# Weight magnitudes on VectorE, new due times, and a second layer turned by VectorE

## The chip, the cores and the metric

One core of one Trainium2 chip runs the whole program. The metric is device time in microseconds of one launch. TensorE (PE) multiplies, VectorE (DVE) and ScalarE (ACT) work elementwise, GpSimd (POOL) does some of the same more slowly, and SyncE (SP) issues most transfers. PEld is TensorE's weight load, which lies beside the multiplication.

## What is computed

A chunked attention, then two two-layer networks over its output, all in fp32 (3072 tokens, width 512, hidden width 2048):

```python
x = attention(q, k, v, mem_k, mem_v)      # chunks of 32, 16 keys to the left, 8 to the right, 8 memory keys
h = x @ moe_w_in                          # 3072 x 512 x 2048
y = softplus(h) @ moe_w_out               # 3072 x 2048 x 512
h = y @ moe2_w_in
out = prelu(h, alpha) @ moe2_w_out        # max(h, 0) + alpha * min(h, 0)
```

The weights arrive as 64-bit floats, seen as pairs of 32-bit words.

## The kernel before

**Three products for one.** Each fp32 operand is split into a high part (fp32r, a rounding copy by ACT) and a low part (the difference, by DVE or POOL). A product is then high*high + high*low + low*high, so that each 128x128x512 block is three matmuls.

**First network** (`schedule`, from line 814). Tokens go in six blocks `b` of 512, the hidden width in 16 slices `f` of 128. A step (b, f) is twelve matmuls `pe_h` into `ps_hh`, softplus on ACT (`act_first`, tile `ta`), the split `high`/`low` (tile `g`), and twelve matmuls `pe_out` into four banks `ps_o`. `SEGMENTS` (line 49) takes blocks 0 and 1 in alternation over slices 0-3, 4-7 and 8-15, so that weights need to be there only as they are used; at the end of a segment the four banks are copied out (`drain_one`, two by ACT and two by DVE, tile `o_sb`) before the next segment's first `pe_out`. Each weight slice comes in two halves of 128x512. A half is loaded (`load_raw`, three `raw` buffers), its magnitude is taken (`magnitude`, ACT function Abs, from the upper words, which lie at a stride of two), it is clamped and turned into fp32 bits by DVE (`clamp`, `convert_a`, `convert_b`, `convert_c`, tile `word`, three buffers), and split by ACT (`high_w`) and POOL (`low_w`) into `wsplit`. The weights of the second network go through the same four steps, also in this stage, and are written to DRAM as operands and sums (`in_ops`, `out_ops`). The attention of 24 tiles of 128 tokens is spread over the stage.

**Order.** All of this is put in order by a planner (`Plan`, lines 84 to 159): every piece has an engine, an assumed duration, what it comes after, the buffers that it takes and gives back, and a due time. Due times are offsets `O` (line 81) from the time of the step that needs the piece. The order that comes out is binding on each engine (`InOrder`, line 60).

**Second network** (`pairs`, line 798). Token blocks go in three pairs `p`. The products of a pair's two halves are made by a Strassen-Winograd scheme of seven products for eight. For each pair, `quad` runs eight times (q = 0 to 7, seven products of six matmuls each, PReLU by ACT and DVE, results `G[0..3, q]`), then `second` runs 56 units n (seven passes of eight). A unit is six matmuls from `g2[n]`, the split of one `G`, into two banks (m = 0, 1). `ready(n)` makes the split: an ACT cast (`high`) and a DVE subtraction (`low`). Its buffers are two of tag `g` and, for every third unit, one of the three `raw` buffers (line 475). In the last quad, `ahead` makes the units 0 to 2 (line 801); unit n makes unit n+2 (line 764). After a pass DVE or ACT put the sums and differences of the banks into `u` and `c` (`after`, line 719). In pairs 0 and 1, POOL adds some `G` by accumulating transfers (`SUMS`); in the last pair DVE adds them. `todo` holds the operands of the next pair, made by DVE and ACT.

**Turning.** A result `c` has hidden outputs on the partitions and tokens along the free axis. `turn` (line 683) transposes it on PE: eight 128x128 transposes into two `acc` banks, one copy by ACT, one by DVE, one transfer of 512 KB. It runs after units 39, 46 and 52, and for the fourth result in the first quad of the next pair (`between`) or, in the last pair, at the end of the program. SP issues in order: `load_w_in` at units 48 and 52 stands behind the output transfers of units 46 and 52.

Of the kernel before, what the change touches and what calls it, by code (L numbers as in the profile page):

```python
# [7 lines left out]
F32 = mybir.dt.float32  # L8
# [8 lines left out]
P = 128  # L17
# [37 lines left out]

A11, A12, A22, S1, S2, S3, S4 = range(7)
# [24 lines left out]
O = {'qo': 32.4, 'km': 28.62, 's': 30.88, 'm': 13.72, 'c': 0.72, 'e': 22.73, 'n': 0.37, 'r': 12.8, 'w': 16.33, 't': 1.22, 'pt': 5.93, 'v': -5.17, 'xh': -11.56, 'xl': 15.24, 'first': 3.34, 'gap': 5.43, 'second': 6.51, 'gap2': 14.3, 'raw': 15.77, 'ab': 7.61, 'cl': 10.42, 'ca': 1.59, 'cb': 4.8, 'cc': -3.37, 'wh': -8.57, 'wl': -26.27, 'odd': 20.31, 'sp': 22.46, 'hi': -4.71, 'lo': 5.91, 'out': 18.4, 'wait': 0.07, 'sloads': 34.06}  # L81
# [81 lines left out]
def attention_mlp_mlp_kernel(ctx: ExitStack, tc, qk, v, w1, w2, consts, out):  # L163
# [473 lines left out]

    def quad(p, q, between, ahead):
# [27 lines left out]
        n0 = halves_of(x1, G[0, q])  # L666
        product(p, n, S4, B22, x4, False)
# [3 lines left out]
        n1 = negative(G[1, q], f0)  # L671
        product(p, n, A22, T4, x3, False)
        prelu(G[1, q], n1, G[1, q])
        dve.scalar_tensor_tensor(out=G[1, q], in0=G[1, q], scalar=-1.0, in1=G[0, q], op0=ALU.mult, op1=ALU.subtract)
        n2 = halves_of(x3, G[2, q])
        minus_prelu(n2, f1, G[2, q])
# [6 lines left out]
    def turn(c, b, d):  # L683

        o = rpool.tile([P, 4, HK], F32, tag="raw", name="o_sb")
        for e in range(2):
            ps = bank(ps_acc, "acc")
            for j in range(2):
                for m in range(2):
                    tok = (2 * e + j) * P  # L690
                    pe.transpose(ps[:, j * HK + m * P:j * HK + (m + 1) * P], c[:, m, tok:tok + P], ident)
            if e:
                dve.tensor_copy(o[:, 2:4, :], ps.rearrange("p (j n) -> p j n", j=2))
            else:
                act.copy(out=o[:, 0:2, :], in_=ps.rearrange("p (j n) -> p j n", j=2))
        sp.dma_start(
            out=out[b * N2:(b + 1) * N2, d * HK:(d + 1) * HK].rearrange("(j p) n -> p j n", p=P), in_=o,
        )

# [5 lines left out]
    def second(p, todo):  # L705

        ps_of, kept, c, later, sums_now = {}, {}, {}, [], []
# [32 lines left out]
        for n in range(7 * NQ):  # L740
# [6 lines left out]
            for m in range(2):  # L747
                for k, (a, e) in enumerate(((0, 0), (0, 1), (1, 0))):
# [32 lines left out]
        return lambda: turn(c.pop((1, 0)), 2 * p, 1)  # L781
# [16 lines left out]
    def pairs(between):  # L798
# [5 lines left out]
        between()  # L804
# [12 lines left out]
    def schedule(when):  # L817
# [13 lines left out]
        for n, k in enumerate(order):  # L831
# [3 lines left out]
            add(("ab", n), "ACT", 0.62, need - O["ab"], lambda k=k: magnitude(0, k), [("raw", n)] + ([("ab", n - 1)] if n else []), ["word"])  # L835
# [89 lines left out]
        for j in range(4 * NQ):  # L925
# [3 lines left out]
            add(("ab2", j), "ACT", 0.62, due - 1, lambda j=j: magnitude(1, halves[j]), [("raw2", j)] + ([("ab2", j - 1)] if j else []), ["word"])  # L929
# [127 lines left out]
```

## Time and profile before

| | us |
|---|---|
| median of 3 runs | 1124.35 (1124.09 to 1126.4) |
| the profiled execution | 1125.37 |
| its span, first to last instruction | 1123.6 |
| TensorE busy | 1079.4 (96%) |
| ScalarE busy | 709.9 (63%) |
| VectorE busy | 686.0 (61%) |
| GpSimd busy | 216.3 (19%) |

The mean granted TensorE clock is 0.988 of full speed. A PE that is counted busy is not PE at its full rate: matmuls are pipelined, so the distance from one start to the next tells the rate. The span falls into the start (attention and the first weights, to about 200 us), the rest of the first network (to 643 us), and the second network (to the end). The rows below are read in that light.

### The profile page before, as it was taken

The numbers are of one execution on the slowest core, as the hardware profiler recorded it, in microseconds if no ns is written. First come the engines' busy times: TensorE is split into PE (matmuls) and PEld (weight loads), VectorE is DVE, ScalarE is ACT, GpSimd is POOL, SyncE is SP. The second block draws the span as 40 slices with busy tenths as digits, with TensorE's granted clock in tenths as the row PEclk, the third lists the DMA queues.
The fourth block names the chain that finished last, engine by engine and source line by source line (L and its number), as shares of the span: only waits on it lengthen the run. The fifth ranks groups of instructions, "written<-read, shape, count | busy, mean of one in ns | idle before, by whom it ended". The sixth has DMA issues, their size and how long they took to land.

```text
span 1123.6 us, 16444 instructions
## 1 busy us (share of the span) xinstructions
PE 1079.4 (96%) x6048; PEld 884.7 (79%) x6048; DVE 686.0 (61%) x1098; ACT 709.9 (63%) x1156; POOL 216.3 (19%) x244
## 2 busy tenths in 40 slices
PE   4798889999999999999999999999999999999998
PEld 3677677888888888888888888788888788888786
DVE  5788876545544543445257256778566768566874
ACT  4789888676766766656566455665455655456543
POOL 0233333333223233333333300000000000000000
PEclk9899989999999999999999999999999999999999
DMA  9864466868666654744446483898565997746802
GB/s 252 259 174 155 153 166 125 194 161 201 177 167 159 177 162 135 209 151 159 132 139 219 145 307 109 314 277 279 191 259 174 352 289 242 263 172 263 323 3 73
DMA packets 157600, 220.83 MB, mean 197 GB/s; under 512 B 73680, under 2 KB 108624, under 8 KB 150608
## 3 DMA queue, kind: packets, MB, share of 16 engines
q1 hardware_dynamic: 153488, 203.00, 55.5%
q0 software_dynamic: 4032, 16.78, 7.8%
q8 instruction: 48, 0.79, 0.3%
q14 instruction: 32, 0.26, 0.1%
HBM read 161.03 MB, written 46.14 MB: 184 GB/s over the span
## 4 chain that ended last, share of the span: by engine, by line
PE 79%; DVE 8%; ACT 7%; DMA 3%; issue 2%; SPq 0%; DVEq 0%; ACTq 0%
PE ps_q L68 35%; PE ps_o L68 20%; PE ps_hh L68 20%; DVE word L68 3%; DMA qk<-in_qk_dram 2%; ACT L68 2%; PE ps_s L68 2%; DVE gb L68 2%; ACT tp L68 2%; PE ps_x L68 2%; DVE g L68 1%; DMA raw<-in_w_dram 1%; ACT g L68 1%; ACT word L68 1%; PE ps_t L68 1%
## 5 line engine op out<-in xcount | busy, mean ns | idle before, releaser
L68 PE MATMUL ps_o<-g,wsplit 128*128 128x512 f32 x1152 | 284.2, 396 | 12.4 <-DVE o_sb L68 9.5
L68 PE MATMUL ps_hh<-x,wsplit 128*128 128x512 f32 x1152 | 283.4, 395 | 1.3 <-DVE x L68 0.8
L68 PEld LDWEIGHTS ps_o<-g,wsplit 128*128 128x128 f32 x1152 | 216.7, 190 | 60.2 <-ACT o_sb L68 10.7
L68 PEld LDWEIGHTS ps_hh<-x,wsplit 128*128 128x128 f32 x1152 | 215.4, 189 | 48.2 <-DVE x L68 1.8
L68 PE MATMUL ps_q<-g,wout 128*128 128x512 f32 x1008 | 233.3, 391 | 2.5 <-DVE g L68 2.3
L68 PE MATMUL ps_q<-xop,win 128*128 128x512 f32 x1008 | 229.7, 389 | 0.0
L68 PEld LDWEIGHTS ps_q<-g,wout 128*128 128x128 f32 x1008 | 188.0, 188 | 43.7 <-DVE g L68 4.5
L68 PEld LDWEIGHTS ps_q<-xop,win 128*128 128x128 f32 x1008 | 189.0, 188 | 39.2
L68 ACT ACT_TABLE_LOAD x120 | 154.0, 1283 | 10.7 <-DVE g L68 6.4
L68 ACT CAST g<-gb 128x512 fp32r<-128x512 f32 x168 | 100.3, 623 | 87.2 <-PE ps_q L68 71.6
L68 DVE TENSOR_TENSOR g<-ta,g 128x512 fp32r<-128x512 f32 x96 | 74.0, 771 | 130.3 <-ACT g L68 129.7
L68 DVE TENSOR_TENSOR g<-gb,g 128x512 fp32r<-128x512 f32 x168 | 113.4, 688 | 45.4 <-ACT g L68 44.5
L68 DVE TENSOR_SCALAR word<-word 128x512 f32<-128x512 f32 (+1 forms) x128 | 63.4, 495 | 89.0 <-ACT word L68 87.4
L68 DVE SCALAR_TENSOR_TENSOR word<-raw,word 128x512 int32<-128x512 int32 x128 | 108.2, 845 | 3.5
L68 ACT CAST g<-ta 128x512 fp32r<-128x512 f32 x96 | 59.3, 618 | 61.6 <-PE ps_o L68 61.1
L68 ACT ACTIVATE ta<-ps_hh 128x512 f32<-128x512 f32 x96 | 57.5, 599 | 59.9 <-PE ps_hh L68 55.2
L68 ACT ACTIVATE tp<-gb 128x512 f32<-128x512 f32 x48 | 30.4, 633 | 90.2 <-DVE gb L68 90.2
L68 POOL TENSOR_TENSOR wst<-wsum,wst 128x512 fp32r<-128x512 f32 x32 | 42.8, 1340 | 136.5 <-ACT wst L68 130.5
L68 DVE SCALAR_TENSOR_TENSOR gb<-gb,tp 128x512 f32<-128x512 f32 x48 | 33.2, 693 | 49.2 <-ACT tp L68 49.2
L68 POOL DMA_DIRECT2D gb<-gb x12 | 10.5, 874 | 267.7 <-DVE g L68 259.6
L68 POOL TENSOR_TENSOR wsplit<-word,wsplit 128x512 fp32r<-128x512 f32 x32 | 45.1, 1413 | 87.5 <-ACT wsplit L68 77.3
L68 POOL TENSOR_TENSOR wst<-word,wst 128x512 fp32r<-128x512 f32 (+1 forms) x32 | 35.2, 1101 | 109.1 <-ACT wst L68 103.7
(72 smaller groups left out, 926.9 us busy)
## 6 DMA issues: line engine op xcount, KB each, us to landing
wout<-out_ops SPq DMA_DIRECT2D x42, 1024.0 KB
raw<-in_w_dram SPq DMA_DIRECT2D x64, 512.0 KB
win<-in_ops SPq DMA_DIRECT2D x24, 1024.0 KB
win<-in_ops SPq DMA_DIRECT2D x24, 768.0 KB
out_ops<-wst SPq DMA_DIRECT2D x56, 256.0 KB
in_ops<-wst SPq DMA_DIRECT2D x24, 512.0 KB
gb<-gb POOLq DMA_DIRECT2D x12, 1024.0 KB, 13.6
qk<-in_qk_dram SPq DMA_DIRECT2D x32, 256.0 KB
```

The lines of the kernel that those rows point to most:

```text
L68: i = getattr(self.engine, name)(*args, **kw)
```

## The change

- `magnitude` is a DVE instruction on integers: a shift left by one and a shift right by one, which clears the sign bit. The planner's entries for it (`ab`, `ab2`) move from ACT to DVE.
- All of `O` is new. Among the offsets: `first` 3.34 to 0.0, `gap` 5.43 to 0.25, `gap2` 14.3 to 2.62, `raw` 15.77 to 26.02, `ab` 7.61 to -1.24, `sp` 22.46 to 17.55, `out` 18.4 to 12.51, `sloads` 34.06 to 18.87.
- `turn` is replaced by `flip` for eleven of the twelve results: DVE transposes 32x32 blocks of `c` in place (two instructions), and eight transfers of 64 KB each, in pieces of 128 bytes, put the blocks where they belong.
- The last result of the last pair goes through `ending`: the m = 1 products of the last three units are put behind all m = 0 products, and the result is turned by PE in one part of four blocks and two parts of two.
- `ready` keeps four units in hand instead of three for the first 20 units (two `g` and two `raw` buffers in turn), and the last quad makes four units ahead (`ahead(3)`).
- In the last quad, the PReLU of `G[1, 7]` and `G[2, 7]` is put off (`rest`): one piece each in the units 0, 1 and 2 of `second`.

```diff
+DEEP = 20
     def magnitude(layer, k):
         m = words[layer, k] = tpool.tile([P, DM], F32, tag="word", name="word", bufs=3)
-        act.activation(out=m, in_=raws[layer, k].bitcast(F32)[:, :, 1], func=AF.Abs)
+        dve.tensor_scalar(
+            out=m.bitcast(I32), in0=raws[layer, k][:, :, 1], scalar1=1, scalar2=1,
+            op0=ALU.logical_shift_left, op1=ALU.logical_shift_right,
+        )
     def high(a, n=0):
-        g = gpool.tile([P, 2, N2], F32R, tag="g", name="g") if n % 3 < 2 else staging("g")
+        g = gpool.tile([P, 2, N2], F32R, tag="g", name="g") if (n % 4 if n < DEEP else (n - DEEP) % 3) < 2 else staging("g")
...
         n0 = halves_of(x1, G[0, q])
+        ahead(3)
         product(p, n, S4, B22, x4, False)
...
-        n1 = negative(G[1, q], f0)
+        if q < NQ - 1:
+            n1 = negative(G[1, q], f0)
         product(p, n, A22, T4, x3, False)
...
+        else:
+            third = []
+            rest[:] = [
+                lambda: second_rest(negative(G[1, q], f0)),
+                lambda: third.append(halves_of(x3, G[2, q])),
+                lambda: minus_prelu(third[0], f1, G[2, q]),
+            ]
...
+    def turn(src, m, j0, n, copy):
+
+        ps = bank(ps_acc, "acc")
+        for j in range(n):
+            pe.transpose(ps[:, j * P:(j + 1) * P], src[:, j * P:(j + 1) * P], ident)
+        o = rpool.tile([P, n, P], F32, tag="raw", name="o_sb")
+        copy(o, ps[:, :n * P].rearrange("p (j n) -> p j n", j=n))
+        tok = (NB - 2) * N2 + j0 * P
         sp.dma_start(
+            out=out[tok:tok + n * P, HK + m * P:HK + (m + 1) * P].rearrange("(j p) n -> p j n", p=P), in_=o,
         )
+    def ending(ps, kept, behind):
+
+        def result(m, part):
+            plus(c[:, m, part], kept["u3", m][:, part], ps[m][:, part], ALU.subtract)
+        c = rpool.tile([P, 2, N2], F32, tag="raw", name="c")
+        result(0, slice(0, N2))
+        for products in behind:
+            products(1)
+        turn(c[:, 0, :], 0, 0, 4, lambda o, i: act.copy(out=o, in_=i))
+        for h in range(2):
+            part = slice(h * HK, (h + 1) * HK)
+            result(1, part)
+            turn(c[:, 1, part], 1, 2 * h, 2, (lambda o, i: act.copy(out=o, in_=i), dve.tensor_copy)[h])
+
+    def flip(c, b, d):
+
+        rows = out[b * N2:(b + 1) * N2, d * HK:(d + 1) * HK].rearrange("(c i) (m a j) -> m a i c j", i=32, m=2, j=32)
+        for m in range(2):
+            o = c[:, m, :].rearrange("p (c i) -> p c i", i=32)
+            dve.transpose(out=o, in_=o)
+            for a in range(4):
+                sp.dma_start(out=rows[m, a], in_=o[32 * a:32 * a + 32])
...
+            products(0)
+            if p == NPAIRS - 1 and n >= 7 * NQ - 3:
+                behind.append(products)
+            else:
+                products(1)
...
-            if 0 < n < 7 * NQ - 2:
-                ready(n + 2)
+            while asked[0] < min(7 * NQ, n + (5 if n < 3 else 4 if n < DEEP - 3 else 3)):
+                ready(asked[0])
+                asked[0] += 1
+            if rest:
+                rest.pop(0)()
...
+            if behind and n == 7 * NQ - 1:
+                ending(ps, kept, behind)
+                return None
...
-                turn(c.pop((d, b)), 2 * p + b, d)
+                flip(c.pop((d, b)), 2 * p + b, d)
...
-        return lambda: turn(c.pop((1, 0)), 2 * p, 1)
+        return lambda: flip(c.pop((1, 0)), 2 * p, 1)
...
-            add(("ab", n), "ACT", 0.62, need - O["ab"], lambda k=k: magnitude(0, k), [("raw", n)] + ([("ab", n - 1)] if n else []), ["word"])
+            add(("ab", n), "DVE", 0.45, need - O["ab"], lambda k=k: magnitude(0, k), [("raw", n)] + ([("ab", n - 1)] if n else []), ["word"])
```

## Rows read from the trace of the kernel before

**Rows 1.** The page, part 1: busy time, share and instructions by engine.
```profile
PE 1079.4 (96%) x6048; PEld 884.7 (79%) x6048; DVE 686.0 (61%) x1098; ACT 709.9 (63%) x1156; POOL 216.3 (19%) x244
```
**Rows 2.** Windows: stretch, length, PE, PEld, DVE, ACT, POOL, PEclk, DMA share, GB/s.
```profile
40.00:100.00 60.00, 53.30 (x410) 41.95 (x410) 48.18 (x85) 52.15 (x85) 21.51 (x23) 0.95 0.67 196
100.00:200.00 100.00, 90.46 (x443) 73.13 (x443) 76.61 (x109) 86.70 (x113) 36.98 (x34) 0.97 0.55 145
200.00:520.00 320.00, 319.85 (x2230) 260.97 (x2229) 151.64 (x270) 213.35 (x339) 96.81 (x119) 1.00 0.64 173
```
**Rows 3.** Waits, 40 to 200 us: who waited for whom; total, times, longest.
```profile
DVE word L68 <- ACT word L68: 23.4, 15, 4.6
...
PE ps_o L68 <- DVE o_sb L68: 9.5, 3, 5.1
...
PE ps_o L68 <- ACT o_sb L68: 2.8, 1, 2.8
```
**Rows 4.** Groups of ACT by form, 40 to 200 us: busy, mean ns, idle before.
```profile
L68 ACT ACT_TABLE_LOAD x44 | 56.5, 1283 | 0.8
L68 ACT ACTIVATE word<-raw 128x512 f32<-128x512 f32 x31 | 20.8, 672 | 1.3 <-DMA raw<-in_w_dram 1.1
```
**Rows 5.** Groups of DVE by form, 40 to 200 us: busy, mean ns, idle before.
```profile
L68 DVE SCALAR_TENSOR_TENSOR word<-raw,word 128x512 int32<-128x512 int32 x64 | 58.2, 909 | 1.4
L68 DVE TENSOR_SCALAR word<-word 128x512 int32<-128x512 int32 x31 | 19.0, 613 | 0.6
...
L68 DVE TENSOR_SCALAR word<-word 128x512 f32<-128x512 f32 x31 | 14.7, 473 | 23.6 <-ACT word L68 23.4
```
**Rows 6.** Timeline of PE, second network: start, length, form, count, idle before.
```profile
651.22 70.90 PE L68 MATMUL ps_q<-xop,win 128*128 128x512 f32 x312
721.96 4.80 PE L68 MATMUL ps_q<-g,wout 128*128 128x512 f32 x19
727.33 17.99 PE L68 MATMUL ps_q<-g,wout 128*128 128x512 f32 x78 [0.57 <-DVE g L68]
...
777.98 1.04 PE L68 MATMUL ps_q<-cst,c 128*128 128x128 f32 x8
778.77 9.82 PE L68 MATMUL ps_q<-g,wout 128*128 128x512 f32 x42
...
802.46 5.61 PE L68 MATMUL ps_q<-xop,win 128*128 128x512 f32 x24
...
879.51 4.49 PE L68 MATMUL ps_q<-g,wout 128*128 128x512 f32 x19
884.54 20.70 PE L68 MATMUL ps_q<-g,wout 128*128 128x512 f32 x90 [0.55 <-DVE g L68]
...
1036.68 4.47 PE L68 MATMUL ps_q<-g,wout 128*128 128x512 f32 x19
1042.33 20.02 PE L68 MATMUL ps_q<-g,wout 128*128 128x512 f32 x87 [1.18 <-DVE g L68]
```
**Rows 7.** Timeline of ACT at the first change from quads to units.
```profile
725.42 1.65 ACT L68 CAST g<-gb 128x512 fp32r<-128x512 f32 x3
```
**Rows 8.** Windows (columns as in rows 2): DVE around unit 39, and two for transfers.
```profile
767.50:788.50 21.00, 20.94 (x97) 16.97 (x96) 20.95 (x35) 11.32 (x21) 0.00 (x0) 1.00 0.73 231
198.10:200.90 2.80, 2.80 (x40) 2.15 (x39) 0.52 (x2) 2.77 (x5) 2.80 (x4) 1.00 1.19 186
...
808.70:811.40 2.70, 2.70 (x15) 2.26 (x13) 1.75 (x4) 1.75 (x4) 0.00 (x0) 1.00 0.00 0
```
**Rows 9.** Timeline of SP's queue around unit 52 of pair 0.
```profile
799.31 0.38 SPq L68 DMA_DIRECT2D out_dram<-o_sb  x1
799.78 1.49 SPq L68 DMA_DIRECT2D win<-in_ops  x2
```
**Rows 10.** Timeline of all engines at the end of the program.
```profile
1112.82 4.34 PE L68 MATMUL ps_q<-g,wout 128*128 128x512 f32 x18
...
1118.96 0.69 DVE L68 COPY o_sb<-ps_q 128x512 f32<-128x512 f32 x1 [1.07 <-PE ps_q L68]
```

More of the change, by code (lines that the diff above doesn't have):

```diff
@@ L80 @@
 RUNS = 8
-O = {'qo': 32.4, 'km': 28.62, 's': 30.88, 'm': 13.72, 'c': 0.72, 'e': 22.73, 'n': 0.37, 'r': 12.8, 'w': 16.33, 't': 1.22, 'pt': 5.93, 'v': -5.17, 'xh': -11.56, 'xl': 15.24, 'first': 3.34, 'gap': 5.43, 'second': 6.51, 'gap2': 14.3, 'raw': 15.77, 'ab': 7.61, 'cl': 10.42, 'ca': 1.59, 'cb': 4.8, 'cc': -3.37, 'wh': -8.57, 'wl': -26.27, 'odd': 20.31, 'sp': 22.46, 'hi': -4.71, 'lo': 5.91, 'out': 18.4, 'wait': 0.07, 'sloads': 34.06}
+O = {'qo': 38.55, 'km': 20.01, 's': 42.81, 'm': 8.58, 'c': 26.31, 'e': 24.49, 'n': -11.6, 'r': 25.75, 'w': -4.38, 't': 6.6, 'pt': 15.86, 'v': 17.47, 'xh': -8.74, 'xl': 10.18, 'first': 0.0, 'gap': 0.25, 'second': 12.27, 'gap2': 2.62, 'raw': 26.02, 'ab': -1.24, 'cl': 13.47, 'ca': 21.21, 'cb': 7.99, 'cc': -20.39, 'wh': -0.17, 'wl': 19.11, 'odd': 7.29, 'sp': 17.55, 'hi': -4.76, 'lo': 24.66, 'out': 12.51, 'wait': 0.15, 'sloads': 18.87}
 class Plan:
@@ L670, in quad, with second_rest @@
         minus_prelu(n0, f0, G[0, q])
-        n1 = negative(G[1, q], f0)
+        if q < NQ - 1:
+            n1 = negative(G[1, q], f0)
         product(p, n, A22, T4, x3, False)
[L673 to L676, printed above, removed]
+        def second_rest(n1):
+            prelu(G[1, q], n1, G[1, q])
+            dve.scalar_tensor_tensor(out=G[1, q], in0=G[1, q], scalar=-1.0, in1=G[0, q], op0=ALU.mult, op1=ALU.subtract)
+        if q < NQ - 1:
+            second_rest(n1)
+            n2 = halves_of(x3, G[2, q])
+            minus_prelu(n2, f1, G[2, q])
+        else:
[5 more added lines that the diff above has]
+            ]
         if q < NQ - 2:
@@ L681, in quad @@
                 load_w_out(14 * p + 2 * (q - NQ + 2) + k)
[L683 to L695, printed above, removed]
+    def turn(src, m, j0, n, copy):
[5 more added lines that the diff above has]
+        tok = (NB - 2) * N2 + j0 * P
         sp.dma_start(
-            out=out[b * N2:(b + 1) * N2, d * HK:(d + 1) * HK].rearrange("(j p) n -> p j n", p=P), in_=o,
+            out=out[tok:tok + n * P, HK + m * P:HK + (m + 1) * P].rearrange("(j p) n -> p j n", p=P), in_=o,
         )
+    def ending(ps, kept, behind):
[17 more added lines that the diff above has]
+                sp.dma_start(out=rows[m, a], in_=o[32 * a:32 * a + 32])
     def ready(n):
@@ L705, in second @@
     def second(p, todo):
-        ps_of, kept, c, later, sums_now = {}, {}, {}, [], []
+        ps_of, kept, c, later, sums_now, asked, behind = {}, {}, {}, [], [], [4], []
         spaces = {S1: (ps_acc, "acc"), A11: (ps_h, "h"), S2: (ps_acc, "acc"), S3: (ps_acc, "acc"), S4: (ps_a, "pa"), A22: (ps_acc, "acc")}
@@ L746, in second, with products @@
             g = g2.pop(n)
-            for m in range(2):
+            def products(m, ps=ps, w=w, g=g, q=q):
                 for k, (a, e) in enumerate(((0, 0), (0, 1), (1, 0))):
@@ L803, in pairs @@
             between = second(p, prepare(p + 1))
-        between()
     first_use = {}
@@ L928, in schedule @@
             dma(("raw2", j), 0.4, 1.9, due - 8, lambda j=j: load_raw(1, halves[j]), [("cv2", j - 1)] if j else [("raw", 2 * NF - 1)], ["raw"])
-            add(("ab2", j), "ACT", 0.62, due - 1, lambda j=j: magnitude(1, halves[j]), [("raw2", j)] + ([("ab2", j - 1)] if j else []), ["word"])
+            add(("ab2", j), "DVE", 0.45, due - 1, lambda j=j: magnitude(1, halves[j]), [("raw2", j)] + ([("ab2", j - 1)] if j else []), ["word"])
             add(("cl2", j), "DVE", 0.46, due, lambda j=j: clamp(1, halves[j], dve), [("ab2", j)])
```

1 line of the change is left out of this document (added).

## The prediction

> **What bounds the kernel now.** First the busy shares: PE is at 96% [rows 1], the other engines far below, so a microsecond is won only where PE stands idle, runs late, or does work that is not a product. Then the windows [rows 2]: from 200 to 520 us PE is busy 319.85 of 320, and no other engine reaches 70%; whatever becomes cheaper for ACT there is worth nothing. PE loses time from 40 to 200 us (53.30 of 60, then 90.46 of 100, and its clock was granted at 0.95 and 0.97). There the other engines are nearly full: ACT 52.15 + 86.70 = 138.9 of 160 us, DVE 124.8. Third the waits there [rows 3]: PE's large ones are for the copies `o_sb` that empty the banks at the ends of the segments, 9.5 + 2.8 = 12.3 us in four waits. DVE in turn waits 23.4 us for the magnitudes from ACT. Fourth the groups of ACT [rows 4]: 44 table loads of 1.283 us take 56.5 us, more than anything else. With 31 magnitudes and a softplus in each step, 44 loads mean that the two functions don't share a table: ACT reloads nearly each time it goes from one to the other. ACT is what everything waits for at the start, and a magnitude costs it not 0.67 us but up to 0.67 + 2 x 1.28. Last, PE's timeline in the second network [rows 6], which gives its rate (312 matmuls between 651.22 and 721.96: 0.2267 us each, 1.36 a unit), the transposes and the stalls.
>
> **The start: magnitudes on DVE and new due times.** Removed from ACT in this stretch: 31 x 0.672 = 20.8 us, and most of the loads. Loads remain where an Exp of the attention comes between softplus; with about five of the 24 tiles in this stretch, some 10 of 44 stay (an estimate), so 34 x 1.28 = 44 us go. ACT falls from 139 to about 75 busy. Added to DVE: 31 magnitudes. No row shows a shift with a strided source. A dense integer shift takes 613 ns here, a dense fp32 clamp 473; the slowest near row, two sources of which one has the same stride, 909 [rows 5]. I take 0.6 us, with 0.47 and 0.91 as bounds: 18.6 us (15 to 28). DVE then has 124.8 + 18.6 = 143 us of work, and the 23.4 us in which it waited for ACT's magnitude are gone, so the new work fits into the hole that its own removal opens. DVE takes ACT's place as the fullest engine: at 93 to 95% busy 143 us need 151 to 154, so of the 160 us some 6 to 9 can go; at 0.91 us a magnitude none can. What goes is the late emptying of the banks: the copies stand in order behind conversions that wait for a magnitude, and behind table loads. The 12.3 us, and the slow clock after the longest waits, bound the gain from above at about 15. The first 40 us I leave unchanged: the order of their first loads is by constants, not by `O`. What new offsets do to the order can't be read from this trace; they can lose as well as win, which is in the range: I take **-7 us, from -14 to +3**. The other half of the magnitudes (after 200 us) lies beside a full PE on a DVE that is 47% busy [rows 2]: nothing.
>
> **Transposes.** Each `turn` puts eight transposes between products: 777.98 to 778.77, 0.79 us [rows 6]. Eleven of twelve go: 11 x 0.79 = **-8.7 us**, on PE's own path, so all of it counts. The copies on ACT and DVE that go with them were beside PE.
>
> **What flip adds on DVE.** Two transposes for one copy, on [128 x 512]. No row has a DVE transpose; the nearest are the 35 instructions between 767.5 and 788.5 us, which fill 20.95 of 21 us [rows 8], 0.60 each when back to back. I take 0.60 each, bounded by half of it and by twice. DVE is full in just the place where the first flip goes (unit 39 starts it): a unit lasts 1.36 us and so has room for 2.27 DVE instructions. Units 39, 40 and 42 have three each (the split, two transposes; the split, a sum, a split for the next pair), units 41 and 43 two. The lag grows by 0.44, 0.44, -0.16, 0.44, to 1.2 us, where before the turn itself gave DVE 0.8 us of pause and one instruction less. By unit 39 the reserve of three units is used up (the sums of units 32 to 37 come before), so I charge PE 1.1 us in pairs 0 and 1: **+2.2 us** (0 to +5 with the transposes at 0.3 or 1.2). In the last pair no operands of a next pair are made, and flips at units 46 and 52 meet a DVE with room: nothing, unless a transpose costs over 1.2.
>
> A sentence from the Trainium skill by itself: VectorE: DVE Perf Modes, section The three transpose paths, gives 311 ns for 128x128 on VectorE in a 16-bit type; as an estimate, with 384 further columns at one per cycle of 0.96 GHz, a [128 x 512] transpose would take 0.71 us, which changes the sum by 0.4 us; no row here shows one.
>
> **What flip adds on the queues.** Eight transfers for one, issued by SP at 0.38 us each as the one before [rows 9]: about 3 us. After unit 39 nothing else waits on SP until `load_w_in` at units 48 and 52. The second stands behind the flip of unit 52, so it goes out 2 to 3 us later than at 799.78. Its data were in by 808.7 (no transfer is active in the next window [rows 8]), and PE takes them up in quad 1, 42 matmuls and a turn after 802.46 [rows 6], at 812.8, some 4 us later. So 512 KB in pieces of 128 bytes may last about 3 us at no cost. Such pieces are in the trace only as loads: the queries of a tile, two transfers of 256 KB in pieces of 32 elements, ran at 186 GB/s with the engines full, 198.1 to 200.9 [rows 8]; the stage's mean, 173 GB/s at a share of 0.64 [rows 2], would be 270 with full engines. At 186 GB/s a flip's data last 2.8 us. I take that for stores, no better and possibly worse: 0. The `raw` buffer of `c` is held from unit 34 to the landing, about six units after 39, and the third `c` comes at unit 48: no wait.
>
> **Change from quads to units.** After 19 matmuls (three units and one), PE stalls: 721.96 + 19 x 0.2267 = 726.27 against 727.33, so 1.06; 0.72 at 879.51 and 1.34 at 1036.68 [rows 6]. The cause is ACT's order: units 3, 4 and 5 are cast at 725.42, in one row [rows 7], behind the last quad's PReLU. With unit 3 made inside the quad and the PReLU in pieces between later units, four units (5.4 us) are in hand. The three pieces add three DVE instructions to units 0 to 2; in the last pair, with splits and sums, that is nine of 0.60 in 4.1 us, a lag of 1.3, which the reserve covers. 3.1 us of stalls become 0.3: **-2.8** (0 to -3.1).
>
> **The end.** The last product ends at 1112.82 + 4.34 = 1117.16 and the span at 1123.6: 6.4 us, of which 3.95 follow the last copy (1119.65) [rows 10]. Now the first half's subtraction lies beside 9 products; after the last product come half a subtraction, two transposes and half a copy, twice overlapped, and smaller transfers: about 1.6 us and then 3. **-1.8** (-2.5 to +1, if the flip of unit 52 is still moving).
>
> **Sum.** -7 - 8.7 + 2.2 - 2.8 - 1.8 = -18.1. Against the profiled execution, 1125.37, that is 1107.3; this one lies 1.0 above the median of the runs, so I give **1106**.
>
> **Rivals.** (a) *DVE becomes the bound of the start.* If a magnitude costs 0.75 to 0.9, or the new order serves them late, DVE has 148 to 153 us to do at a share that it doesn't keep, and the start stays as it was or loses 3: 1113 to 1116. For it: DVE's 124.8 already, and conversions that last 909 ns on the mean in this stretch, where DVE instructions of that size go at 0.60 in the second network [rows 5, 8]. Against: the 23.4 us. (b) *Slow small stores*, which ends slower than before. Let a flip's data last F. Twice the second operands of the next pair come F - 1.5 late, and the last flip stands before the last stores by F - 4: 2(F - 1.5) + (F - 4) = 3F - 7. It eats the 18 us from F = 8.4 us, three times the load rate, and at four times (11.2 us, longer than the 8 us between flips) it gives 1106 + 26.6 = 1133. For it: the pieces are an eighth of the 1 KB before, so eight times as many. Against: loads of that size keep two thirds of the mean rate. The Trainium skill (DMA: Bandwidth & Descriptors, Specifications) speaks for it: below 512 bytes a transfer does read-modify-write and misses the line rate. By that rule a flip at twice the cost lasts 5.6 us and the time would be 1116, not slower than before; the trace agrees for loads, 186 GB/s against 270, and shows no such store. (c) *The start gains all of its stalls*, 14 us: 1099. (d) *The change doesn't do what it says*: the stalls at the change of stage only move to later units, since DVE is full there; then 2.8 us less: 1109, inside the range.
>
> **How the numbers follow.** The forecast with (d) has 0.62; (a) 0.18; (c) 0.11; (b), beyond its break-even, 0.09, and that is the chance of slower. The range reaches over (a) with a twice slower store, to 1119, and down to 1094, the lower bounds of the start and the end together. A measurement of this kernel tells about 0.2%, 2.2 us, from no change. Faster 0.87, same 0.04 (the tail of (a)), slower 0.09.
>
> **What would show it.** After: no magnitude and about a third of the 120 table loads on ACT; DVE over 90% from 40 to 200 us and PE's waits for `o_sb` under 5 us (else rival a); eight transposes on PE instead of 96; no stall over 0.3 us at 19 matmuls after a quad; a stall of about 1 us near units 40 to 43 of pairs 0 and 1; 5 us or less after the last product. The forecast is wrong if PE waits for `win` in quad 1 (rival b), if a DVE transpose takes over 1.2 us, or if the stretch up to 40 us grows.

## The result, and the profile after

| | before | after |
|---|---|---|
| median of 4 runs each, us | 1124.22 (1123.65 to 1126.4) | 1099.49 (1095.99 to 1100.22) |
| ratio | | 0.977, 95% interval 0.9746 to 0.9795 |
| span of the profiled execution | 1123.6 | 1097.7 |

The change makes the kernel 2.3% faster. 1106 was forecast, with a range of 1094 to 1119 and a chance of 0.87 for faster: the side is right and the time lies in the range, but 6.5 us below the forecast. The 25.9 us by which the span shrank can be divided among the stages, as the sum of the prediction was. Each row is read from one trace of before and one of after:

| term | forecast, us | measured, us | read from |
|---|---|---|---|
| start | -7 (-14 to +3) | -17.1 | the block of 312 matmuls begins at 634.10, not 651.22 |
| eleven transposes on PE | -8.7 | -8.7 | none left between products |
| DVE's lag after `flip` | +2.2 | +2.0 | stalls of 1.23 a pair, where before had 0.235 |
| queues | 0 | +0.3 | one wait for `win` |
| change from quads to units | -2.8 | -2.1 | 2.97 gone, 0.82 come back at unit 7 of the last pair |
| flips of the last pair | 0 | +0.4 | the flip of unit 52 delays one split |
| end | -1.8 | -0.8 | 6.4 to 5.6 after the last product |
| sum | -18.1 | -26.0 | span: -25.9 |

So one term was far off, by 10 us, and the others nearly cancel: from the first unit of pair 0 to the end of the last product the second network took 395.2 us before (721.96 to 1117.16, [rows 6, 10]) and 387.3 after (704.82 to 1092.09), that is -7.9 for terms that sum up to -8.1. The stalls are counted by the late matmul alone. The matmul next behind a stall or a transpose starts some 0.1 us late as well; these add up to 1.6 us in before and 1.9 in after, so they hardly touch the sum.

How exact is the row of the start? Nine of the traces below share after's first network (after, e3, e5, e6, e7, e8, e10, e12, e13), and in them the 312 matmuls begin anywhere from 630.8 to 636.9. Most of that spread lies ahead of the first step: its first `pe_h` matmul starts between 34.6 and 41.5. Counted from that matmul, the 312 begin after 595.4 to 597.6 us in all nine, 595.7 in after, and after 613.3 in before (37.91 to 651.22). So the start's gain is 17.6 us by this count, good to some 2 us, and nothing of it comes from the time ahead of the first step.

The page of after, part 1, answers to [rows 1]. ACT lost 146 us of work, and PE 15 us, while DVE gained 34:

```profile
PE 1064.6 (97%) x5960; PEld 871.2 (79%) x5960; DVE 720.0 (66%) x1174; ACT 563.8 (51%) x1000; POOL 219.8 (20%) x244
```

Windows of after (columns as in [rows 2]). The first is the start as it is now, 40 to 184 us: from 184 us on PE is full up to the 312 matmuls, as it was in before from 200 us on. The others answer to [rows 2]. PE went from 53.30 to 54.51 and from 90.46 to 98.10, its clock from 0.95 and 0.97 to 1.00, ACT from 138.9 to 82.1 in sum, DVE from 124.8 to 144.6:

```profile
40.00:184.00 144.00, 136.61 (x874) 111.04 (x873) 134.83 (x226) 75.16 (x133) 64.43 (x57) 1.00 0.68 184
40.00:100.00 60.00, 54.51 (x433) 44.06 (x432) 56.33 (x102) 38.57 (x71) 25.52 (x25) 1.00 0.71 204
100.00:200.00 100.00, 98.10 (x542) 80.05 (x541) 88.31 (x140) 43.52 (x75) 45.00 (x41) 1.00 0.65 170
```

Waits of PE in after, 40 to 184 us, against [rows 3]: 12.3 us for the copies that empty the banks have become 1.9.

```profile
PE ps_o L71 <- DVE o_sb L71: 1.9, 3, 1.0
PE ps_t L71 <- ACT pt L71: 1.7, 1, 1.7
```

Groups of after by form. ACT's table loads from 40 to 200 us (against [rows 4]: 44, 56.5 us); then DVE from 40 to 184 us, conversion and magnitude (against [rows 5]: the conversion 909 ns); then DVE's transposes over the whole program:

```profile
L71 ACT ACT_TABLE_LOAD x9 | 11.5, 1283 | 0.2
...
L71 DVE SCALAR_TENSOR_TENSOR word<-raw,word 128x512 int32<-128x512 int32 x64 | 55.6, 869 | 0.9
...
L71 DVE TENSOR_SCALAR word<-raw 128x512 int32<-128x512 int32 x32 | 18.1, 564 | 0.8 <-DMA raw<-in_w_dram 0.7
...
L71 DVE STREAM_TRANSPOSE c<-c 128x512 f32<-128x512 f32 x22 | 14.3, 686 | 0.0
```

Timeline of PE in after, second network (against [rows 6]). There is no `cst,c` row before the last one, 235 matmuls go without a break after the quads of pair 0, and the small breaks near units 39 to 45 of that pair (pair 1 has the like), and those at unit 7 and before the last units of the last pair, are what is left:

```profile
634.10 70.88 PE L71 MATMUL ps_q<-xop,win 128*128 128x512 f32 x312
...
704.82 53.56 PE L71 MATMUL ps_q<-g,wout 128*128 128x512 f32 x235
758.54 1.65 PE L71 MATMUL ps_q<-g,wout 128*128 128x512 f32 x6 [0.15 <-DVE g L71]
760.35 4.64 PE L71 MATMUL ps_q<-g,wout 128*128 128x512 f32 x18 [0.16 <-DVE g L71]
765.14 15.13 PE L71 MATMUL ps_q<-g,wout 128*128 128x512 f32 x64 [0.15 <-DVE g L71]
...
1014.06 10.07 PE L71 MATMUL ps_q<-g,wout 128*128 128x512 f32 x43
1024.79 64.22 PE L71 MATMUL ps_q<-g,wout 128*128 128x512 f32 x282 [0.66 <-DVE g L71]
1089.29 2.80 PE L71 MATMUL ps_q<-g,wout 128*128 128x512 f32 x11 [0.28 <-DVE g L71]
```

The number in brackets is what the row counts as idle. A stall is longer than that, since the profile models the end of the matmul before it. From start to start, the break ahead of 1024.79 is 1.05 us where 0.227 is usual, so the stall is 0.82.

### The profile page after: what moved, and what is told of

The parts are those of the page before. It is cut to its first block, busy times and chain, and to the rows that moved or that the text cites. A ratio compares the mean times of both kernels' runs of the same rounds, so it can differ in the third digit from the quotient of the medians.

```text
span 1097.7 us, 16278 instructions
## 1 busy us (share of the span) xinstructions
PE 1064.6 (97%) x5960; PEld 871.2 (79%) x5960; DVE 720.0 (66%) x1174; ACT 563.8 (51%) x1000; POOL 219.8 (20%) x244
## 4 chain that ended last, share of the span: by engine, by line
PE 80%; DVE 10%; DMA 5%; issue 2%; ACT 2%; SPq 0%; DVEq 0%; ACTq 0%
PE ps_q L71 36%; PE ps_o L71 20%; PE ps_hh L71 20%; DVE word L71 5%; DMA qk<-in_qk_dram 3%; DVE g L71 2%; PE ps_s L71 2%; PE ps_x L71 2%; DMA raw<-in_w_dram 1%; PE ps_t L71 1%; DVE c L71 1%; DVE gb L71 1%; DMA win<-in_ops 1%; ACT tp L71 1%; SPq L71 0%
## 5 line engine op out<-in xcount | busy, mean ns | idle before, releaser
L71 PE MATMUL ps_o<-g,wsplit 128*128 128x512 f32 x1152 | 280.5, 392 | 1.9 <-DVE o_sb L71 1.9
L71 PE MATMUL ps_hh<-x,wsplit 128*128 128x512 f32 x1152 | 280.2, 392 | 0.7 <-ACT x L71 0.5
L71 PEld LDWEIGHTS ps_o<-g,wsplit 128*128 128x128 f32 x1152 | 214.0, 188 | 48.0 <-ACT ta L71 1.4
L71 DVE TENSOR_SCALAR word<-word 128x512 f32<-128x512 f32 (+1 forms) x128 | 67.6, 530 | 2.0
L71 ACT CAST g<-ta 128x512 fp32r<-128x512 f32 x96 | 59.6, 621 | 17.6 <-PE ps_o L71 15.4
L71 POOL TENSOR_TENSOR wsplit<-word,wsplit 128x512 fp32r<-128x512 f32 x32 | 48.9, 1533 | 64.3 <-ACT wsplit L71 64.3
```

The lines of the kernel that those rows point to most:

```text
L71: i = getattr(self.engine, name)(*args, **kw)
```

## The experiments

Times are medians of device time; the ratio is to the kernel before, run beside each. The diffs of the first four are against before, the others against after.

| kernel | us | ratio (95%) | span |
|---|---|---|---|
| e1: magnitude on DVE, old due times | 1113.57 | 0.9898 (0.9877 to 0.9919) | 1111.2 |
| e2: new due times, Abs on ACT | 1133.37 | 1.0071 (1.0052 to 1.009) | 1131.1 |
| e3: both | 1107.78 | 0.9843 (0.9822 to 0.9864) | 1106.1 |
| e4: Copy for Abs on ACT | 1108.81 | 0.9851 (0.9833 to 0.9869) | 1107.1 |
| after | 1099.49 | 0.977 (0.9746 to 0.9795) | 1097.7 |
| e5: turned by PE again | 1107.17 | 0.9847 (0.9832 to 0.9863) | 1104.5 |
| e6: three units in hand | 1101.98 | 0.9799 (0.9785 to 0.9813) | 1098.8 |
| e7: differences of y on POOL | 1098.45 | 0.9766 (0.9744 to 0.9788) | 1097.7 |
| e8: other buffers at the end | 1098.69 | 0.9772 (0.9758 to 0.9786) | 1096.0 |
| e9: one signed clamp | 1104.96 | 0.9814 (0.9792 to 0.9835) | 1104.3 |
| e10: DVE's pieces spread | 1094.79 | 0.973 (0.9717 to 0.9743) | 1094.9 |
| e12: e10 and e8 | 1093.83 | 0.9731 (0.9717 to 0.9745) | 1089.5 |
| e13: every flip stored twice | 1133.34 | 1.007 (1.0049 to 1.009) | 1134.0 |

### The start: e1 to e4

**e1**, the magnitude moved, `O` as before:

```diff
-        act.activation(out=m, in_=raws[layer, k].bitcast(F32)[:, :, 1], func=AF.Abs)
+        dve.tensor_scalar(
+            out=m.bitcast(I32), in0=raws[layer, k][:, :, 1], scalar1=1, scalar2=1,
+            op0=ALU.logical_shift_left, op1=ALU.logical_shift_right,
+        )
```

> The kernel before, with the magnitudes alone moved to DVE (instruction and planner entry); the old offsets stay. Theory 1 (ACT's table reloads set the pace of the start, the magnitudes on ACT cause them): table loads fall from 120 to about 40, the second network begins 8 to 15 us earlier than at 651.2, time 1109 to 1116. Theory 2 (the new offsets did it, by putting the emptying of the banks earlier): within 4 us of 1124. Theory 3 (DVE becomes the bound unless the order is fitted to it): 1124 or slower.

**e2**, `O` replaced, nothing else:

```diff
-O = {'qo': 32.4, 'km': 28.62, 's': 30.88, ...
+O = {'qo': 38.55, 'km': 20.01, 's': 42.81, ...
```

> The kernel before with the new offsets alone; the magnitudes stay on ACT. Theory 1: the table loads stay near 120 and ACT stays over 85% busy from 40 to 200 us, so at most 4 us are won, and an order fitted to another split of work may lose: 1120 to 1130. Theory 2: 12 to 17 us faster, 1107 to 1112.

**e3**, the edits of e1 and e2 together; the second network is that of before.

> The kernel before with both, the second network untouched. All theories: the 17 us by which the second network begins earlier in the changed kernel, 1106 to 1109. If it is slower than that, some of the 17 us comes from the second network's edits. The difference to the run with the magnitudes alone is what the offsets add once DVE has the magnitudes: theory 1 says 2 to 7 us.

**e4**, before with one word changed. The magnitude stays on ACT, in the same place of the same order, reading the same strided words; the sign stays in the word:

```diff
-        act.activation(out=m, in_=raws[layer, k].bitcast(F32)[:, :, 1], func=AF.Abs)
+        act.copy(out=m, in_=raws[layer, k].bitcast(F32)[:, :, 1])
```

> The kernel before with a copy in place of the magnitude, still on ACT, in the same order: the sign of the weights is not cleared, so that part of the computation is left out. The instruction costs ACT the same 0.6 us, but a copy needs no table. Theory 1 in its narrow form (the reloads, not the 0.67 us, are the cost): table loads fall to about 40, 8 to 14 us faster, 1110 to 1116. Rival (what matters is that DVE no longer waits for another engine, or the order): under 4 us faster, 1120 to 1125.

e3 gives 17.5 us of span, the whole of the start's gain; e1 alone 12.4, and e2 alone loses 7.5. So the new due times are worth 5 to 6 us where DVE has the magnitudes (1113.57 against 1107.78), and cost 8 to 9 where ACT has them: what the due times are worth depends on who makes the magnitudes. e2's trace shows before's picture again. Windows 40 to 100, waits of PE and table loads of ACT, 40 to 200 us:

```profile
40.00:100.00 60.00, 52.20 (x400) 41.81 (x399) 48.71 (x82) 52.53 (x84) 19.96 (x21) 0.89 0.64 181
...
PE ps_o L68 <- DVE o_sb L68: 11.3, 4, 5.7
...
L68 ACT ACT_TABLE_LOAD x41 | 52.6, 1283 | 1.3 <-DVE sm L68 0.4 <-DVE v L68 0.2
```

e4 says what the gain is made of. With no work moved and no due time touched, it takes 16.5 us off the span. Its table loads from 40 to 200 us fell from 44 to 8, and DVE's waits for the magnitude from 23.4 to 6.6:

```profile
L68 ACT COPY word<-raw 128x512 f32<-128x512 f32 x32 | 21.0, 657 | 4.9 <-DMA raw<-in_w_dram 2.8 <-POOL wsplit L68 1.9
L68 ACT ACT_TABLE_LOAD x8 | 10.3, 1283 | 0.4 <-DVE sm L68 0.2
...
DVE word L68 <- ACT word L68: 6.6, 6, 2.7
```

The copies themselves cost ACT as much as the Abs did (21.0 against 20.8 us [rows 4]). What went is 36 loads. Before's own timeline of ACT shows the pattern that is removed: softplus (`ta<-ps_hh`) and Abs (`word<-raw`) in turn, a load in front of each:

```profile
122.46 1.28 ACT L68 ACT_TABLE_LOAD   x1
123.75 0.60 ACT L68 ACTIVATE ta<-ps_hh 128x512 f32<-128x512 f32 x1
124.37 1.28 ACT L68 ACT_TABLE_LOAD   x1
125.66 0.70 ACT L68 ACTIVATE word<-raw 128x512 f32<-128x512 f32 x1
```

The loads' removal by itself therefore brings nearly the whole gain of the start, shown by e4: 15.6 us from the first `pe_h` matmul to the 312 (36.97 to 634.69), of the 17.6 of after. Moving the magnitude to DVE was one way to be rid of the loads. By time e3, which does that with new due times, is not told apart from e4, which leaves a function on ACT that needs no load and keeps the old ones (1107.78 and 1108.81, overlapping intervals).

### Is DVE the bound of the start now? e9

In after DVE is busy 134.83 of 144 us, 94%. The magnitude and the clamp after it, both on DVE, are replaced by one clamp with both signs:

```diff
-        dve.tensor_scalar(
-            out=m.bitcast(I32), in0=raws[layer, k][:, :, 1], scalar1=1, scalar2=1,
-            op0=ALU.logical_shift_left, op1=ALU.logical_shift_right,
-        )
+        dve.tensor_scalar(out=m, in0=raws[layer, k].bitcast(F32)[:, :, 1], scalar1=-DBL_MOST, scalar2=DBL_MOST, op0=ALU.max, op1=ALU.min)
```

> The kernel after with less work for VectorE at the start: one clamp with both signs, straight from the raw words, takes the place of magnitude and clamp (weights smaller in size than the least convertible one are no longer raised to it, so that part of the computation is left out). About 31 x 0.47 to 0.56 us = 15 to 17 us of VectorE's 135 busy microseconds between 40 and 184 us go. Theory 'VectorE is now the bound of the start': at the 94% that it keeps, the 312 matmuls of the first quads begin some 8 to 15 us earlier than 634, less what the attention, the loads or PE itself then hold back; PE is busy for 132 of these 144 us, so 4 to 10 us: 1090 to 1096. Rival 'the start is now bound by PE itself and by the loads of weights': under 2 us, 1097 to 1100.

Both expectations missed: 1104.96 is above both, and above after, though the two intervals against before just touch. Windows of e9:

```profile
40.00:184.00 144.00, 135.66 (x847) 110.33 (x847) 126.62 (x194) 75.41 (x131) 62.27 (x57) 0.96 0.65 178
60.00:80.00 20.00, 16.16 (x119) 12.96 (x117) 16.75 (x29) 11.98 (x25) 6.69 (x7) 0.83 0.49 152
```

DVE has 8 us less to do, and not the 15 to 17 that were expected, in part because its conversions took 933 ns each where after has 869. PE is not earlier: the 312 matmuls begin at 639.10, 5.0 us later than in after, and 600.6 us after the first `pe_h` matmul, 3 us beyond the nine traces of after's first network. The planner put a DVE instruction of 0.46 us less into its plan and made another order of it, with a hole of PE between 60 and 80 us in which the clock was granted at 0.83. Here a lighter DVE gained nothing; since the order changed with it, the run by itself doesn't say that DVE is no bound. e4 adds to it: there DVE is busy 125.74 us from 40 to 184, in an order of its own, and the 312 matmuls begin at 634.69, where after has 634.10. So the same start was reached with a DVE that has 9 us less to do. Whether DVE bounds after's own order, and whether due times made for e9 would bring a gain, stays open.

### The second network: e5, e6, e7, e10

**e5**, the eleven results turned by PE as in before (`whole` is the old `turn`); everything else of after stays:

```diff
-                flip(c.pop((d, b)), 2 * p + b, d)
+                whole(c.pop((d, b)), 2 * p + b, d)
```

> The changed kernel with the eleven results turned by PE as before (eight transposes, two copies, one transfer of 512 KB); the special end stays. Theory (the transposes stood on PE's path and flip's price is DVE's two instructions): 8.7 us of transposes come back, of the 2.5 us of stalls near units 38 to 43 of pairs 0 and 1 about 2 go: 1105 to 1107. Rival (flip's small stores delay loads and cost a few us): 1103 or less.

It costs 7.7 us by the medians, 6.8 by the spans, and 6.2 from the begin of the 312 matmuls to the last product's start (463.79 for 457.60), which leaves the spread of the start out. The account has 8.7 of transposes less 2.0 of stalls, 6.7. In its timeline of pair 0 the rows of transposes are back, and the stalls near unit 39 are down to one of 0.32:

```profile
705.40 53.57 PE L71 MATMUL ps_q<-g,wout 128*128 128x512 f32 x235
759.12 1.43 PE L71 MATMUL ps_q<-g,wout 128*128 128x512 f32 x5
760.39 1.04 PE L71 MATMUL ps_q<-cst,c 128*128 128x128 f32 x8
761.18 9.83 PE L71 MATMUL ps_q<-g,wout 128*128 128x512 f32 x42
```

**e6**, three units in hand and the last quad's PReLU undivided, as in before:

```diff
-        g = ... if (n % 4 if n < DEEP else (n - DEEP) % 3) < 2 else staging("g")
+        g = ... if n % 3 < 2 else staging("g")
...
-        ahead(3)
...
-            while asked[0] < min(7 * NQ, n + (5 if n < 3 else 4 if n < DEEP - 3 else 3)):
-                ready(asked[0])
-                asked[0] += 1
+            if 0 < n < 7 * NQ - 2:
+                ready(n + 2)
```

> The changed kernel with three units in hand and the last quad's PReLU undivided, as before; flip and the special end stay. Theory (the stalls of 3.1 us at 19 matmuls after a quad were ACT's order): they come back, the 0.8 us at unit 7 of the last pair goes: 1101 to 1103. Rival (the stalls only move, DVE is full there): 1099 to 1100.

It costs 2.5 us by the medians and 1.1 by the spans, and its interval overlaps that of after, so the time alone doesn't settle it. The timeline does: from the begin of the 312 matmuls to the last product's start it takes 2.0 us more than after. The stall after 19 matmuls is back in each pair (0.69, 0.72 and 1.31 us from start to start beyond the usual 0.227), and that at unit 7 of the last pair is gone; PE, last pair of e6:

```profile
1014.57 4.51 PE L71 MATMUL ps_q<-g,wout 128*128 128x512 f32 x19
1020.22 69.69 PE L71 MATMUL ps_q<-g,wout 128*128 128x512 f32 x306 [1.15 <-DVE g L71]
```

So the stall at unit 7 is the old one put off: the last pair's DVE has the splits, the sums of `G` and the three PReLU pieces in units 0 to 2, and falls behind by more than the one unit that was added.

**e7**, the differences of y, that DVE makes among the splits, by POOL from pair 1 on:

```diff
-        dve.tensor_tensor(out=y_raw[p, h, to], ...
+        (pool if p else dve).tensor_tensor(out=y_raw[p, h, to], ...
```

> The changed kernel with the four differences of the next pair's operands (units 33 to 37, and the same of the first half) made by POOL instead of DVE. Theory (DVE is full from unit 32 to 45 of pairs 0 and 1, and PE's five short stalls there, 1.2 us a pair, are its lag): DVE has four instructions, 2.4 us, less there; the stalls go, 1097 to 1098.5. Rival (POOL's work slows DVE's, or comes late itself): 1099 or more.

No difference to after can be told by the time. Pair 0 still stalls, now in two larger breaks, while pair 1's are mostly gone; PE, pair 0 of e7:

```profile
755.68 4.67 PE L71 MATMUL ps_q<-g,wout 128*128 128x512 f32 x18 [0.26 <-DVE g L71]
760.99 14.22 PE L71 MATMUL ps_q<-g,wout 128*128 128x512 f32 x57 [0.64 <-DVE g L71]
```

One pair speaks for DVE's load as the cause of the stalls and one against, so this run doesn't settle it. **e10** leaves the work on DVE and only puts it at other units:

```diff
-                for at, k, e in ((0, 1, 3), (10, 0, 1), (26, 1, 2)):
+                for at, k, e in ((3, 1, 3), (10, 0, 1), (26, 1, 2)):
...
-            todo[at] = [lambda h=h: load_y(p, h)]
...
+        for h, load, sums, last, splits in ((0, 1, (8, 9, 10), 12, (11, 13, 15, 17, 19, 21, 23)), (1, 26, (33, 35, 37), 44, (38, 45, 47, 48, 49, 50, 51))):
```

> The kernel after with the work on y for the second half put at other units (its sums at units 33, 35 and 37 and its splits from 45 on, so that only one stands in the stretch of units 38 to 43 where a flip lies), and with the last pair's sums of G begun at unit 3 instead of 0. Theory 'the stalls near units 38 to 43 (1.2 us in each of pairs 0 and 1) and the one at unit 7 of the last pair (0.8 us) are VectorE's lag behind several pieces put close together': both go, about 3 us, 1096 to 1097. Rival 'the pieces only move, and VectorE lags elsewhere (units 33 to 37, where the sums meet banks of a pass, or units 45 to 51)': 1098.5 to 1100.

1094.79: 4.7 us below after, and the two intervals against before don't overlap. The stall at unit 7 is gone (325 matmuls without a break), pair 1 has none, and pair 0 keeps one; PE of e10, pair 0 and the last:

```profile
758.75 11.55 PE L71 MATMUL ps_q<-g,wout 128*128 128x512 f32 x47 [0.58 <-DVE g L71]
...
1012.29 73.85 PE L71 MATMUL ps_q<-g,wout 128*128 128x512 f32 x325
1086.42 2.79 PE L71 MATMUL ps_q<-g,wout 128*128 128x512 f32 x11 [0.28 <-DVE g L71]
```

From the begin of the 312 matmuls to the last product's start it takes 453.45 us, after 457.60: -4.15. The stalls account for 2.3 of it: 3.3 in after (twice 1.23 and 0.82) against 1.0 that stays in pair 0. The rest is after's wait for `win`, 0.3, and for the most part the matmuls next behind the stalls, 1.9 us in after and 0.5 in e10.

### The end and the queues: e8, e12, e13

**e8** takes the buffers of the end's copies from the first network's tiles:

```diff
-        o = rpool.tile([P, n, P], F32, tag="raw", name="o_sb")
+        o = tpool.tile([P, n, P], F32, tag="tb" if j0 else "ta", name="o_sb", bufs=1 if j0 else 2)
```

> The changed kernel with the three copies of the end put into buffers that no flip holds. Theory (the second copy waited 0.8 us for the transfer of the flip before it, which still held a raw buffer): 0.5 to 0.9 us faster at the end, which is little more than can be told; the profile must show the copy without that wait. Rival (the last transfers stand behind the flip's pieces in the queues anyway): the end stays at 5.6 us after the last product.

In after, the second copy at the end waited for the flip's transfers, which held a `raw` buffer. In e8 the copies follow each other. First the row of after, then that of e8:

```profile
1093.94 0.37 ACT L71 COPY o_sb<-ps_q 128x256 f32<-128x256 f32 x1 [0.79 <-DMA out_dram<-c]
```

```profile
1091.10 0.89 ACT L71 COPY o_sb<-ps_q 128x512 f32<-128x512 f32 x2 [5.34 <-PE ps_q L71]
```

But what follows the last product went from 5.6 to 5.3 us only: of the 0.79 us of waiting 0.3 counted, and the time is that of after. In after the last copy, the row above, ends 2.2 us after the last product, and 3.4 us of transfers follow it. In e8 these are 1.7 and 3.6. **e12**, e10 with these buffers:

> The same spread, and the copies of the last result in buffers of the first network's tiles rather than in raw ones, of which the flip of unit 52 holds one. By the theory that the 0.79 us wait of the second copy at the end is for that buffer, and that the stalls are VectorE's lag: 0.5 to 1 us less than the spread alone, 1095.5 to 1096.5. Rival: the end is bound by the store of the last piece, whatever buffer it leaves from: the same as the spread alone.

1093.83, the lowest, and not told apart from e10. In pair 0 its PE has no break at all, and between pair 1 and the next quads it waits for `win`:

```profile
701.54 76.40 PE L71 MATMUL ps_q<-g,wout 128*128 128x512 f32 x336
...
930.93 9.36 PE L71 MATMUL ps_q<-xop,win 128*128 128x512 f32 x40 [0.58 <-DMA win<-in_ops]
```

**e13** asks how much room there is behind the flips. Each transfer is followed by a copy of itself to a spare place in DRAM:

```diff
                 sp.dma_start(out=rows[m, a], in_=o[32 * a:32 * a + 32])
+                sp.dma_start(out=more[m, a], in_=o[32 * a:32 * a + 32])
```

> The kernel after with every flip's eight transfers followed each by a copy of itself to a spare place in DRAM: twice the pieces of 128 bytes, twice SP's issues (16 for a flip), the same work on DVE. It measures the room behind the flips. The formula of the prediction's rival on slow stores, 3F - 7, with F doubled from the 3.6 us that a flip's data take in the kernel after, gives 14.6 us: 1114. Theory from the kernel after: the loads of win behind the flips are the only ones who wait; one stall of 0.34 us for win stands already at the end of pair 1, so the room there is about nothing, and each flip that lies ahead of a load adds its 4 us to it: 4 to 8 us in each of pairs 0 and 1 and up to 4 at the end: 1108 to 1116, with PE waiting for win at the first quads of pairs 1 and 2. Rival, that the queue has room for all of it and the 0.34 us is chance: under 2 us, 1097 to 1101.5.

1133.34: 34 us above after, and above before by 0.7%. All three expectations lay below it. Waits of PE from 600 us on, PE's timeline at the first quads of pair 1, and a window just behind the wait of 4.76 us:

```profile
PE ps_q L71 <- DMA win<-in_ops: 16.5, 6, 4.8
...
789.21 9.82 PE L71 MATMUL ps_q<-xop,win 128*128 128x512 f32 x42 [2.02 <-DMA win<-in_ops]
803.79 12.12 PE L71 MATMUL ps_q<-xop,win 128*128 128x512 f32 x42 [4.76 <-DMA win<-in_ops]
817.74 59.08 PE L71 MATMUL ps_q<-xop,win 128*128 128x512 f32 x252 [1.83 <-DMA win<-in_ops]
...
804.00:807.00 3.00, 3.00 (x8) 2.32 (x9) 0.00 (x0) 0.25 (x1) 0.00 (x0) 0.50 1.16 259
```

In each of the two pairs the loads of three quads are late, 8.6 and 7.9 us of waiting. After the first wait, of 2.02 us, the 42 matmuls of the next row run at their usual distance (9.82 us). After each of the other five PE runs at the lower of its two levels for a while (0.50, that is 1.2 of 2.4 GHz: 8 matmuls in 3 us). From the begin of the 312 matmuls to the last product's start it took 28.4 us more than after, of which 16.5 are waits and some 9 are lost by matmuls at the lower level. What follows that start takes 5.0 more, because the last flip's stores stand ahead of the end's.

What holds the loads up is SP. It issues in order, and from 764.99 to 811 it hardly rests: a flip's sixteen issues, one every 0.55 us, take 8.8 us, where 8.2 lie between the flips of units 46 and 52 (six units of 1.36). The loads for the first two quads of pair 1 leave at 783.41 and 798.18, and PE's waits for them end at 789.21 and 803.79. In after these loads leave at 775.99 and 786.71. First two rows of SP in e13 and one of after, then DMA in e13 from 740 to 820 us, in 40 slices of 2 us (busy share in tenths, and GB/s):

```profile
783.41 1.18 SPq L71 DMA_DIRECT2D win<-in_ops  x2
798.18 1.18 SPq L71 DMA_DIRECT2D win<-in_ops  x2
```

```profile
786.71 1.18 SPq L71 DMA_DIRECT2D win<-in_ops  x2
```

```profile
DMA  9999999999999967777777799947788999776999
GB/s 279 285 381 436 262 260 289 291 291 262 270 410 430 281 93 118 119 121 118 120 121 118 113 376 389 230 59 118 121 97 291 398 303 146 118 123 111 350 395 418
```

Where the flips' pieces move alone, at 118 to 121 GB/s (64 KB in 0.55 us is 119), the engines are not full: 7 tenths. So in these stretches SP's issuing sets the pace and not the stores. The run doubled SP's issues together with the pieces, so it doesn't tell what slower stores alone would cost.

## Why the prediction was right and where it was wrong

**What bounds the kernel.** The reading that PE loses its time from 40 to 200 us, and that ACT's table loads are behind it, holds: e4 took away the loads and nothing else of weight, and got 16.5 us of span.

**The start, the term that was mis-sized.** -7 was forecast, -17.1 came, outside the term's own range of -14 to +3; rival (c), 14 us at a chance of 0.11, was the nearest. Its parts were right one by one: a magnitude takes 0.56 us there (0.6 taken), 9 loads remain of 44 (10 estimated), ACT is busy 82 us from 40 to 200 (75), DVE 94% from 40 to 184 (93 to 95). The step that failed is the one behind them: DVE was made the engine that sets the pace, and its 143 us of work at that share were turned into a time. In the stretch that the gain shortens, 40 to 184 us, DVE did 134.8 us of work and not 143, since part of what it did up to 200 us isn't needed by then, and its conversions got shorter (869 for 909 ns). And PE doesn't follow DVE's load: in e4 DVE is busy 125.74 in the same 144 us, in e3 136.69, in after 134.83, in e9 126.62, while PE is busy 137.70, 137.47, 136.61 and 135.66 (in e9 at a clock of 0.96). Windows 40 to 184 us of e3 and then of e4:

```profile
40.00:184.00 144.00, 137.47 (x877) 111.63 (x877) 136.69 (x228) 74.75 (x132) 63.75 (x55) 1.00 0.68 183
```

```profile
40.00:184.00 144.00, 137.70 (x856) 112.05 (x857) 125.74 (x194) 88.08 (x160) 59.01 (x57) 0.99 0.68 182
```

A better sum stood in the rows: what PE lost in the stretch was the 12.3 us of waits and a clock of 0.95 over 60 and 0.97 over 100 us, 3 + 3 us of slower work [rows 2, 3]; with the waits at 1.9 and the clock at 1.00 that gives 10.4 + 6 = 16.4 (an estimate made with the result in hand), against 17.1. The prediction named this bound ("at about 15", which the result passed by 2 us) and then took half of it by the utilisation of another engine.

**Rival (a)** didn't come: a magnitude took 0.56 us and not 0.75 to 0.9, the new order didn't serve them late, and the stretch got shorter by all that PE had lost. That new due times "can lose as well as win" was right to the letter: e2 lost 7.5 us and e1 to e3 won 5, by the same edit.

**Transposes, and DVE's lag.** -8.7 and +2.2 against -8.7 and +2.0, and e5, at 6.2 to 7.7 us, agrees with their sum. The price of a DVE transpose, taken from the nearest rows at 0.60, is 0.69 by the group. That the lag is one of order and not of load is shown by e10, which with the same work removes it from pair 1 and leaves 1.0 us in pair 0, and by e12, where with the same order pair 0 has none either. For the last pair nothing was forecast, on a DVE with room; its flip of unit 52 delays a split and costs 0.4.

**Change from quads to units.** -2.8 was forecast with rival (d), that the stalls move, beside it at 2.8 less; the truth lies between: they are gone in two pairs, and in the last one 0.82 of 1.3 us moved to unit 7. The step that failed is that "the reserve covers" a lag of 1.3 us from nine DVE instructions in 4.1 us: the splits and the sums of `G` went on from there. With these sums begun three units later (e10) the stall is gone.

**The end.** -1.8 became -0.8, within its range (-2.5 to +1). Of the two parts, 1.6 us to the last copy became 2.2, and 3 us of transfers became 3.4. Not seen was that the copies' buffers are `raw` ones and that the flip of unit 52 still held one; but e8 shows that this cost 0.3 us only. What sets the 3.6 us of transfers that e8 still has was not tried.

**The queues, right with less room than was thought.** The flips cost 0.3 us, as good as the nothing that was forecast. Window of after in which the 4096 pieces of one flip, 512 KB, move beside little else:

```profile
793.10:796.70 3.60, 3.60 (x18) 2.98 (x17) 2.55 (x4) 3.17 (x6) 0.00 (x0) 1.00 1.00 161
```

F is thus 3.6 us where 2.8 was taken, and rival (b) didn't come. The Trainium skill (DMA: Bandwidth & Descriptors, Specifications) has transfers under 512 bytes miss the line rate by read-modify-write. Here such stores ran at 161 GB/s with the engines full, against 186 for loads in pieces of that size [rows 8] and the 270 that the prediction estimated for full engines: the trace agrees that they miss the line rate, and shows no doubling against loads.

What the prediction had wrong here is SP. Eight issues were to take about 3 us; they take 4.1 when nothing holds them up, longer than the data with full engines:

```profile
1088.13 4.13 SPq L71 DMA_DIRECT2D out_dram<-c  x8
```

Against the first product of the next quads, the load at unit 52 leaves 6.3 us later than in before (3.65 us after it, 786.71 to 783.06; before 2.68 ahead of it, 799.78 to 802.46 [rows 6, 9]), where 2 to 3 were forecast. The load at unit 48, for which no delay was forecast, leaves 4.6 us later, behind sixteen issues of two flips, and after's one wait for `win` is for such a load (0.3; in e12 0.7). So the room was used up; that the flips cost no more is in part luck. The formula of rival (b) counts data alone: at F = 7.2 it gives 14.6 us, and e13, which doubles SP's issues too, cost 33.4 in the stages that it touches. Its break-even, F = 8.4 us, is tested by no run, but the chance of 0.09 for slower leant on more room than there was.

## What to carry to other kernels

Where two functions of ACT are in turn and each is preceded by a table load, get one of them off its table first (to another engine, or to a function that needs no load) and time that alone: here that brought nearly all of a stage's 17 us. When the wait that holds the bound engine is removed, sum up what that engine lost (its waits, and the slow clock after them) rather than a share of the engine that is next fullest. And before small pieces of work or small transfers are added to a nearly full queue or engine, count the time to issue them beside the time of their data, and measure the room by doubling them: here the flips were nearly free once, and twice as many stores cost more than the whole change had saved. The same pieces of work, a few units further apart, may cost less, as in e10.

## What the runs showed of the hardware

- Abs and softplus don't share a table, and Copy needs none of its own: 44 loads in 160 us with Abs, 8 with Copy in its place (e4). A load lasts 1.28 us and the next instruction begins some 0.01 us after it (122.46 + 1.28 to 123.75).
- A DVE instruction on integers whose source has a stride of two words took 0.56 us for 128x512 between 40 and 184 us, as much as a dense one there (0.59), and less than one with two sources (0.87).
- SP needs about 0.5 us to issue a transfer of 64 KB in 512 pieces, so 4.1 us for a flip when nothing holds it up (1088.13 in after). With such transfers alone in e13 that made 118 to 121 GB/s, at an engines' share of 7 tenths.
- After a wait of 4.76 us PE's granted clock stood at 0.50 in the next 3 us, so that wait cost more than its own length.
